# New engine orders and engine choices for windowed attention followed by an RWKV channel mix

## The chip, the cores and the metric

The kernel runs on one core of a Trainium2 chip. The core has TensorE (PE, matmuls), VectorE (DVE), ScalarE (ACT), GpSimd (POOL) and SyncE (SP, which here only issues transfers), and 16 DMA engines that move data between HBM and the on-chip memory SBUF. Matmul results land in PSUM banks. The metric is the device time of one execution in microseconds; a version's time is the median of its runs.

## The reference

Attention over 4 batches, 8 heads, 768 positions and head size 64. Every query sees the 128 newest keys and the first 4 (the sinks). Its output, heads side by side, is the input x of a channel mix with width 512 and hidden width 1024. The core of it:

```python
scores = scale * np.matmul(q, k.transpose(0, 1, 3, 2))
keep = is_sink | in_window
scores = np.where(keep, scores, -1000000000.0)
a = np.exp(scores - np.max(scores, axis=-1, keepdims=True))
a = a / (np.sum(a, axis=-1, keepdims=True) + 1e-09)
attn = np.matmul(a, v)
# x = attn as (B, S, 512); x_prev = x one position earlier
xk = mu_k * x + (1.0 - mu_k) * x_prev
xr = mu_r * x + (1.0 - mu_r) * x_prev
k = np.maximum(xk @ w_k, 0.0)
v = k * k @ w_v
r = 1.0 / (1.0 + np.exp(-(xr @ w_r)))
return r * v
```

Inputs and output are float32 in HBM. The kernel computes in bf16 and accumulates in float32.

## The kernel before

**Tiling.** The 4 x 768 positions are cut into 12 units u of 256 rows, three to a batch, so u = 0, 3, 6, 9 begin a batch. For each unit the functions below append operations to a list, in a fixed order of construction; an operation's place in it is its number (0 to 1030), and those numbers are all that the two tables at the top of the file hold.

- `load` (L386): SP transfers of k, q and v of a unit, into three buffers each. k from unit 4 on and q from unit 8 on come in two halves (L403), the others in one (L410); v comes in halves (L393). `load_weight` (L418): 1 MB each, two for wk, one for wr, two for wv.
- `cast` (L553): a weight to bf16 in pieces of 128 x 1024 (wk four pieces 81 to 84, wr 85 and 86, wv 87 to 90).
- `prepare` (L586): k and q of a unit to bf16 (L594, L597), then transposed so that the head dimension lies on the partitions. Early units do it on PE (four transposes, L623) with an evacuation from PSUM (L631); k from unit 4 on and q from unit 8 on by a transposing transfer on SP (L610). v goes to bf16 (L645). At the start of a batch also the sink keys (L662, POOL) and sink values (L668, L672).
- `attend` (L678): scores of two head pairs at a time in two wide PSUM tiles (L708; for units 0 and 1 a bias is first put there by matmuls, L715), exponentials on ACT (L744), the mask as a product on DVE for units from 2 on (L758), sink scores and their exponentials (L685, L692), values (L770, L782), then reciprocal and scaling into x on DVE (L795, L798).
- `mix` (L807): x transposed on PE (L821), evacuated to xt (L830), the difference of neighbouring positions td (L848), and from it xk and xr (L859).
- `ffn` (L898): keys xk times wk (L909, eight groups of four products), ReLU (L919 or L923), square to kk (L936 or L932), gate xr times wr (L948) and its tanh (L954), kk times wv (L966), the two multiplied into ob (L975) and stored by SP (L982). The last half unit is in two parts (`last_product`, L869).

**What sets the order.** Nothing is scheduled at run time. `ORDER` (L54) lists, for each engine, the numbers of its operations in the order in which the engine runs them, and an engine waits at the head of its list until that operation's inputs and buffers are there. `CHOICE` (L18) gives the engine of an operation that has alternatives: casts of k, q, v (ACT, DVE or POOL), evacuations (ACT or DVE), ReLU and square (ACT or DVE), weight casts. `Plan.schedule` (L163) walks the lists with a table of estimated durations. It decides which buffer each operation takes (four PSUM banks in the pool `bank`, two wide tiles `sc`, five tiles `e`, and so on) and where filler matmuls on a tile of zeros (L986) go into PE's list while it expects PE to be idle, before 32 us of its own clock.

The operations that the prediction speaks of:

| number | what | engine before |
|---|---|---|
| 19; 258, 260 | load of k of unit 3; cast of its first half; its evacuation kt[3,0] | SP; ACT, ACT |
| 259 | PE transposes of k of unit 3, first half | PE |
| 227; 309, 310; 313, 314 | products with wv: unit 0, second half of rows 0 to 127; unit 1, rows 0 to 127 and rows 128 to 255, two halves each | PE |
| 292, 296 | squares kk[1,0], kk[1,1] | ACT, DVE |
| 93, 96; 136 | evacuations kt[0,0], qt[0,0]; kt[1,1] | DVE, ACT; ACT |
| 120, 124; 131 | exponentials of unit 0; cast of q of unit 1 | ACT |
| 158, 159; 161 | bias and scores of unit 1; values of unit 1 | PE |
| 81; 82 | casts of wk, first and second piece | DVE; ACT |
| 206, 207; 210, 211; 214 | keys of unit 0, groups 0, 1 and 2 | PE |
| 234, 192; 175 | sink scores of unit 2; transposes of x of unit 1; values of unit 1 | PE |
| 200; 208, 212; 184; 180 | evacuation of xt; ReLUs of unit 0; cast of k and evacuation kt[2,0] | ACT |
| 236; 317; 443 | scores of unit 2 and of unit 3; first keys of unit 3 | PE |
| 392; 928, 994 | stores of ob of units 2, 9 and 10 | SP |
| 738, 857; 883 | sink keys of the last batch; sink scores of unit 10; cast of q of unit 11 | POOL, PE; ACT |
| 1015, 1019, 1020 | gate and products of unit 11, rows 0 to 127 | PE |

Of the kernel before, what the change touches and what calls it, by code (L numbers as in the profile page):

```python
# [18 lines left out]
    82: "ACT", 83: "ACT", 89: "ACT", 93: "DVE", 97: "DVE", 99: "DVE", 100: "DVE", 102:  # L19
    "DVE", 103: "ACT", 104: "ACT", 133: "DVE", 139: "DVE", 140: "DVE", 141: "DVE", 150:  # L20
    "DVE", 178: "DVE", 181: "DVE", 190: "DVE", 191: "DVE", 209: "ACT", 264: "DVE", 266:
    "DVE", 270: "ACT", 271: "DVE", 283: "DVE", 292: "ACT", 300: "ACT", 341: "DVE", 349:
    "ACT", 352: "DVE", 359: "DVE", 368: "ACT", 372: "ACT", 379: "DVE", 380: "ACT", 417:
    "DVE", 427: "DVE", 428: "DVE", 446: "ACT", 458: "ACT", 495: "POOL", 497: "DVE", 505:
    "DVE", 527: "ACT", 531: "ACT", 535: "ACT", 539: "ACT", 574: "DVE", 581: "DVE", 583:
    "DVE", 584: "DVE", 585: "ACT", 603: "ACT", 660: "ACT", 661: "ACT", 670: "DVE", 679:
    "ACT", 687: "ACT", 728: "DVE", 730: "DVE", 732: "DVE", 736: "ACT", 737: "ACT", 758:
    "ACT", 762: "ACT", 766: "ACT", 770: "ACT", 809: "DVE", 813: "DVE", 814: "ACT", 816:
    "DVE", 823: "DVE", 832: "ACT", 885: "DVE", 890: "ACT", 899: "DVE", 912: "ACT", 915:
    "DVE", 916: "ACT", 920: "ACT", 974: "ACT", 978: "ACT", 986: "ACT", 1002: "ACT", 1006:  # L30
    "ACT", 1013: "DVE", 1014: "ACT",
# [24 lines left out]
        92, 95, 108, 109, 79, 101, 98, 118, 119, 111, 125, 106, 121, 115, 158, 132, 129,  # L56
        142, 135, 138, 159, 182, 149, 156, 188, 168, 169, 165, 234, 161, 175, 206, 207,
        171, 192, 210, 211, 199, 218, 214, 219, 179, 215, 185, 236, 293, 289, 301, 297,
        290, 298, 302, 294, 247, 239, 244, 224, 222, 305, 275, 307, 250, 230, 255, 231,
        226, 282, 262, 227, 259, 268, 309, 317, 265, 310, 313, 342, 328, 314, 365, 369,  # L60
        366, 373, 347, 374, 370, 320, 325, 395, 331, 336, 383, 377, 351, 378, 381, 358,
        273, 393, 406, 385, 389, 420, 386, 390, 443, 425, 451, 444, 452, 398, 473, 409,
        403, 447, 414, 448, 455, 429, 456, 484, 471, 436, 498, 461, 459, 467, 476, 468,
        524, 528, 525, 529, 481, 503, 552, 487, 536, 492, 537, 463, 510, 508, 464, 532,
        517, 563, 533, 555, 540, 560, 542, 548, 577, 549, 586, 600, 604, 601, 566, 605,
        571, 630, 608, 582, 609, 544, 593, 612, 545, 613, 616, 628, 641, 618, 633, 676,
        638, 677, 688, 680, 689, 681, 662, 684, 644, 649, 704, 706, 685, 620, 669, 621,
        624, 717, 694, 625, 755, 692, 756, 759, 763, 709, 760, 764, 714, 783, 720, 696,
        725, 741, 697, 739, 700, 748, 701, 767, 794, 786, 773, 771, 768, 791, 779, 829,
        833, 830, 802, 780, 834, 841, 815, 842, 837, 775, 797, 838, 776, 845, 822, 859,  # L70
        857, 847, 853, 849, 854, 850, 862, 870, 867, 905, 909, 906, 913, 891, 910, 914,
        923, 917, 873, 918, 878, 921, 933, 935, 898, 925, 929, 926, 930, 946, 971, 938,
        943, 972, 975, 979, 976, 980, 957, 983, 949, 984, 954, 987, 989, 964, 995, 991,
        996, 992, 999, 1003, 1000, 1007, 1004, 1011, 1015, 1008, 1012, 1019, 1017, 1020,
# [3 lines left out]
        69, 70, 93, 100, 97, 80, 99, 102, 112, 113, 126, 107, 122, 116, 127, 117, 123,  # L78
        133, 181, 139, 144, 140, 150, 145, 147, 151, 141, 152, 146, 155, 153, 81, 162,
        166, 163, 176, 148, 167, 177, 172, 173, 84, 194, 195, 178, 201, 196, 203, 202,  # L80
        197, 217, 154, 221, 86, 190, 238, 243, 191, 85, 204, 198, 240, 205, 245, 241, 213,
        246, 249, 87, 88, 254, 90, 251, 304, 252, 256, 277, 257, 280, 232, 296, 283, 278,
        284, 228, 264, 279, 281, 288, 341, 266, 286, 319, 285, 324, 311, 315, 335, 271,
        330, 287, 321, 326, 322, 376, 332, 327, 337, 333, 338, 397, 352, 379, 417, 353,
        359, 274, 360, 354, 402, 356, 355, 362, 361, 387, 391, 408, 357, 413, 364, 399,
        400, 410, 404, 411, 405, 363, 497, 415, 454, 416, 427, 431, 450, 475, 434, 432,
        438, 428, 433, 440, 439, 435, 477, 480, 469, 478, 486, 491, 505, 482, 441, 488,
        483, 489, 493, 494, 559, 574, 554, 442, 465, 509, 519, 512, 556, 557, 561, 513,
        562, 514, 521, 520, 565, 515, 550, 570, 581, 567, 523, 568, 572, 584, 516, 573,
        583, 522, 588, 632, 589, 607, 637, 595, 590, 597, 596, 546, 728, 634, 591, 635,  # L90
# [948 lines left out]
```

## Time and profile before

| | |
|---|---|
| median of 8 runs | 167.73 us (167.48 to 168.15) |
| profiled execution, time | 167.32 us |
| profiled execution, span from first to last instruction | 165.4 us |
| PE busy | 157.7 us, 1614 matmuls recorded |
| DVE, ACT busy | 141.8 and 139.4 us |
| POOL busy | 12.7 us |
| moved by DMA | 33.81 MB, mean 204 GB/s |
| TensorE clock granted | full speed in every slice |
| chain that ended last | PE 72%, SP's queue 17%, DMA 7% |

The span is what the profile sees; the time of the same execution is 1.9 us longer. Busy time is the sum of an engine's instructions; for PE their ends are modelled, so gaps are read from the starts. Engines' instructions are named by line, operation and tiles, and a wait is put down to what released it. In the timeline a bracket holds the idle time before a row and who ended it.

### The profile page before, as it was taken

What the parts mean: (1) busy time and instruction counts of PE and PEld (TensorE: products, weight loads), DVE (VectorE), ACT (ScalarE), POOL (GpSimd) and SP (SyncE); (2) the same over time, 40 slices, a digit from 0 to 9 for tenths busy, and PEclk for the clock granted to TensorE, in tenths of its full rate; (3) what the DMA queues carried; (4) which work ended last, traced back from release to release, by engine and by line L of the source; (5) the groups of instructions that cost most, each with busy time, mean ns of one, the idle gap of its engine ahead of it and who ended that gap; (6) DMA issues with size and microseconds to landing.
All of it is one profiled execution on the core that took longest, in us unless ns stands there. A gap on an engine that the chain in (4) does not pass through costs nothing.

```text
span 165.4 us, 4222 instructions
## 1 busy us (share of the span) xinstructions
PE 157.7 (95%) x1614; PEld 107.1 (65%) x1632; DVE 141.8 (86%) x369; ACT 139.4 (84%) x234; POOL 12.7 (8%) x39
## 2 busy tenths in 40 slices
PE   7999789998999999999999999999999999999992
PEld 5657478754577578586585874855765685684761
DVE  5459899999998999999999899889799898978441
ACT  3589999997999999999999899988967799676550
POOL 7800000000100120040000001000000200000000
PEclk9999999999999999999999999999999999999999
DMA  4999999999969989999899698999849952110303
GB/s 139 242 282 256 370 351 266 334 350 270 259 135 283 223 217 234 176 213 251 196 206 235 138 185 245 213 262 261 171 75 258 250 134 111 73 58 0 127 0 127
DMA packets 81762, 33.81 MB, mean 204 GB/s; under 512 B 63688, under 2 KB 76240, under 8 KB 81744
## 3 DMA queue, kind: packets, MB, share of 16 engines
q1 hardware_dynamic: 81728, 33.56, 81.8%
q8 instruction: 12, 0.20, 0.5%
q14 instruction: 6, 0.05, 0.1%
q10 hardware_dynamic: 16, 0.00, 0.0%
HBM read 24.12 MB, written 6.29 MB: 184 GB/s over the span
## 4 chain that ended last, share of the span: by engine, by line
PE 72%; SPq 17%; DMA 7%; issue 1%; ACT 0%; DVE 0%
PE bank L966 22%; PE bank L909 21%; PE bank L948 10%; DMA ks<-in_k_dram 7%; SPq L428 6%; SPq L393 6%; PE sc L708 6%; PE bank L782 5%; SPq L410 4%; PE bank L821 3%; PE bank L770 2%; PE bank L623 2%; PE bank L879 1%; PE bank L685 1%; PE bank L668 0%
## 5 line engine op out<-in xcount | busy, mean ns | idle before, releaser
L909 PE MATMUL bank<-xk,wk_sb 128*128 128x256 bf16 x384 | 49.9, 273 | 0.5 <-DVE wk_sb L565 0.5
L744 ACT ACTIVATE e<-sc 128x1024 bf16<-128x1024 f32 (+1 forms) x48 | 44.6, 964 | 4.7 <-PE sc L708 4.6
L966 PE MATMUL bank<-wv_h,kk 128*128 128x512 bf16 x174 | 43.8, 379 | 0.6 <-issue 0.2
L909 PEld LDWEIGHTS <-wk_sb 128*128 128x128 bf16 x384 | 35.5, 98 | 8.3 <-DVE wk_sb L565 0.6
L919 ACT ACTIVATE rl<-bank 128x512 bf16<-128x512 f32 x45 | 26.1, 606 | 7.2 <-PE bank L909 6.8
L966 PEld LDWEIGHTS <-kk 128*128 128x128 bf16 x184 | 17.0, 98 | 16.2 <-issue 0.2
L758 DVE TENSOR_TENSOR e<-e,mask 128x1024 bf16<-128x1024 bf16 (+1 forms) x40 | 25.7, 653 | 0.1
L948 PE MATMUL bank<-wr_sb,xr 128*128 128x512 bf16 x88 | 23.4, 379 | 0.4
L859 DVE SCALAR_TENSOR_TENSOR xr<-td,mu_all,xt 128x256 bf16<-128x256 bf16 x48 | 23.2, 488 | 0.0
L859 DVE SCALAR_TENSOR_TENSOR xk<-td,mu_all,xt 128x256 bf16<-128x256 bf16 x48 | 21.7, 478 | 0.1
L798 DVE TENSOR_TENSOR x<-bank,rec 128x256 bf16<-128x256 f32 x48 | 19.2, 414 | 0.3
L782 PE MATMUL bank<-vb,e 128*128 128x65 bf16 x352 | 19.5, 193 | 0.0
L782 PEld LDWEIGHTS <-e 128*128 128x128 bf16 x352 | 16.7, 98 | 2.9 <-ACT e L744 0.9
L936 ACT ACTIVATE kk<-rl 128x512 bf16<-128x512 bf16 x29 | 18.0, 631 | 0.6 <-DVE rl L923 0.6
L975 DVE SCALAR_TENSOR_TENSOR ob<-th,bank 128x512 f32<-128x512 f32 x23 | 15.5, 682 | 2.4 <-ACT th L954 1.6
L954 ACT ACTIVATE th<-bank 128x512 f32<-128x512 f32 x24 | 14.2, 603 | 1.4 <-PE bank L948 1.1
L708 PE MATMUL sc<-qt,kt 64*128 64x128 bf16 (+1 forms) x256 | 13.9, 238 | 0.6 <-ACT kt L631 0.4
L795 DVE RECIPROCAL rec<-bank 128x4 f32<-128x4 f32 x48 | 8.2, 176 | 6.7 <-PE bank L782 6.1
L948 PEld LDWEIGHTS <-xr 128*128 128x128 bf16 x96 | 8.6, 98 | 7.8
L770 PE MATMUL bank<-vsink,es 128*128 128x130 bf16 x64 | 12.6, 221 | 0.0
L708 PEld LDWEIGHTS <-kt 64*128 64x128 bf16 x256 | 9.0, 94 | 5.4 <-issue 2.0
L830 ACT COPY xt<-bank 128x512 bf16<-128x512 bf16 x16 | 9.4, 589 | 1.4 <-DVE vsink L672 1.1
(72 smaller groups left out, 172.5 us busy)
## 6 DMA issues: line engine op xcount, KB each, us to landing
vs<-in_v_dram SPq DMA_DIRECT2D x24, 256.0 KB, 4.5
out_dram<-ob SPq DMA_DIRECT2D x23, 256.0 KB, 3.3
ks<-in_k_dram SPq DMA_DIRECT2D x18, 256.0 KB, 4.8
qs<-in_q_dram SPq DMA_DIRECT2D x7, 512.0 KB, 5.7
qs<-in_q_dram SPq DMA_DIRECT2D x10, 256.0 KB, 4.4
w<-in_moe_w_k_dram SPq DMA_DIRECT2D x2, 1024.0 KB, 8.2
w<-in_moe_w_v_dram SPq DMA_DIRECT2D x2, 1024.0 KB, 8.5
ks<-in_k_dram SPq DMA_DIRECT2D x3, 512.0 KB, 8.9
```

What stands on the lines that cost most here:

```text
L708: nc.tensor.matmul(out=sc[:, a, o0:o1], lhsT=lhs[rows], rhs=rhs[rows], start=u not in BIAS, stop=True, skip_group_check=u in BIAS)
L744: nc.scalar.activation(out=buf[ek][:, :, lo:], in_=buf[sck][:, :, lo:], func=AF.Exp, scale=scale)
L758: nc.vector.tensor_tensor(out=at, in0=at, in1=m, op=ALU.mult)
L770: nc.tensor.matmul(out=o[:, g, :, :], lhsT=buf["es", u][:, 128 * g:128 * g + 128], rhs=vsink[b % 2][:, 2 * c:2 * c + 2, :], start=True, st ...
L782: nc.tensor.matmul(out=o[:, g, a, :], lhsT=e[:, a, e0:e0 + 128], rhs=rhs, start=(T == 0 and i == 0), stop=(i == len(blocks) - 1), skip_gro ...
L798: P.op("DVE", dve(256), lambda ok=ok, rk=rk, c=c: nc.vector.tensor_tensor(out=buf["x", u][:, :, 128 * c:128 * c + 128].rearrange("p g (a d ...
L859: nc.vector.scalar_tensor_tensor(out=buf[key][:, c0 + i, :], in0=buf[tk][:, i, :], scalar=mu[w][:, c0 + i:c0 + i + 1], in1=xt[:, c0 + i, t ...
L909: nc.tensor.matmul(out=ps[:, i, :], lhsT=wk_sb[:, c, 128 * f:128 * f + 128], rhs=xk[:, c, :], start=(c == 0), stop=(c == NC - 1), skip_gro ...
L919: nc.scalar.activation(out=buf[rk], in_=buf[psk].rearrange("p (i t) -> p i t", i=2), func=AF.Relu)
L936: nc.scalar.activation(out=buf["kk", u][:, 2 * f2:2 * f2 + 2, :], in_=buf[rk], func=AF.Square)
L948: nc.tensor.matmul(out=buf[psk], lhsT=buf["xr", u][:, c, 128 * g:128 * g + 128], rhs=wr_sb[:, c, :], start=(c == 0), stop=(c == NC - 1))
L966: nc.tensor.matmul(out=buf[psk], rhs=wv_h[:, f, :], lhsT=buf["kk", u][:, f, 128 * g:128 * g + 128], start=(f == 0), stop=(f == NF - 1))
```

## The change

Both tables are replaced. No other line differs: the operations, their dependences, the tiles and the loops are the same, so each engine runs the same kinds of instructions on the same shapes. 75 operations change their engine: 29 casts of q, k and v, one weight cast (81), 15 evacuations, 5 ReLUs and 25 squares. Most trade places between ACT and DVE (31 go to DVE, 32 to ACT; of the squares 12 and 13); ten casts go to POOL, seven from ACT and three from DVE, and two leave POOL. ACT has 230 operations after 235, DVE 354 after 357, POOL 24 after 16; PE (307) and SP (116) have the same ones in another order. The diff, cut within the long lists:

```diff
 CHOICE = {
-    82: "ACT", 83: "ACT", 89: "ACT", 93: "DVE", 97: "DVE", 99: "DVE", 100: "DVE", 102:
-    "DVE", 103: "ACT", 104: "ACT", 133: "DVE", 139: "DVE", 140: "DVE", 141: "DVE", 150:
-    "DVE", 178: "DVE", 181: "DVE", 190: "DVE", 191: "DVE", 209: "ACT", 264: "DVE", 266:
-    "DVE", 270: "ACT", 271: "DVE", 283: "DVE", 292: "ACT", 300: "ACT", 341: "DVE", 349:
-    "ACT", 352: "DVE", 359: "DVE", 368: "ACT", 372: "ACT", 379: "DVE", 380: "ACT", 417:
-    "DVE", 427: "DVE", 428: "DVE", 446: "ACT", 458: "ACT", 495: "POOL", 497: "DVE", 505:
-    "DVE", 527: "ACT", 531: "ACT", 535: "ACT", 539: "ACT", 574: "DVE", 581: "DVE", 583:
-    "DVE", 584: "DVE", 585: "ACT", 603: "ACT", 660: "ACT", 661: "ACT", 670: "DVE", 679:
-    "ACT", 687: "ACT", 728: "DVE", 730: "DVE", 732: "DVE", 736: "ACT", 737: "ACT", 758:
-    "ACT", 762: "ACT", 766: "ACT", 770: "ACT", 809: "DVE", 813: "DVE", 814: "ACT", 816:
-    "DVE", 823: "DVE", 832: "ACT", 885: "DVE", 890: "ACT", 899: "DVE", 912: "ACT", 915:
-    "DVE", 916: "ACT", 920: "ACT", 974: "ACT", 978: "ACT", 986: "ACT", 1002: "ACT", 1006:
-    "ACT", 1013: "DVE", 1014: "ACT",
+    81: "POOL", 82: "ACT", 83: "ACT", 89: "ACT", 93: "DVE", 96: "DVE", 99: "DVE", 100:
+    "DVE", 103: "DVE", 104: "ACT", 134: "POOL", 136: "DVE", 137: "DVE", 139: "DVE", 140:
+    "ACT", 141: "ACT", 143: "DVE", 150: "DVE", 178: "DVE", 187: "POOL", 189: "DVE", 190:
+    "DVE", 191: "DVE", 258: "DVE", 271: "DVE", 283: "DVE", 292: "ACT", 296: "ACT", 304:
+    "ACT", 341: "DVE", 343: "DVE", 344: "DVE", 349: "ACT", 352: "DVE", 359: "DVE", 368:
+    "ACT", 376: "ACT", 380: "ACT", 417: "POOL", 424: "POOL", 427: "ACT", 428: "DVE", 430:
+    "DVE", 446: "ACT", 454: "ACT", 458: "ACT", 495: "POOL", 497: "DVE", 506: "DVE", 535:
+    "ACT", 539: "ACT", 579: "DVE", 584: "DVE", 585: "ACT", 594: "DVE", 607: "ACT", 611:
+    "ACT", 615: "ACT", 652: "POOL", 660: "ACT", 661: "ACT", 663: "DVE", 687: "ACT", 691:
+    "ACT", 728: "DVE", 730: "DVE", 732: "DVE", 736: "DVE", 737: "ACT", 758: "ACT", 766:
+    "ACT", 770: "ACT", 813: "DVE", 814: "DVE", 816: "DVE", 832: "ACT", 836: "ACT", 840:
+    "ACT", 844: "ACT", 881: "DVE", 883: "POOL", 887: "POOL", 889: "ACT", 890: "ACT", 892:
+    "DVE", 899: "DVE", 920: "ACT", 974: "ACT", 982: "ACT", 1002: "ACT", 1005: "DVE", 1006:
+    "ACT", 1009: "DVE", 1010: "ACT", 1014: "ACT",
 }
...
     "PE": (
-        92, 95, 108, 109, 79, 101, 98, 118, 119, 111, 125, 106, 121, 115, 158, 132, 129,
-        142, 135, 138, 159, 182, 149, 156, 188, 168, 169, 165, 234, 161, 175, 206, 207,
-        171, 192, 210, 211, 199, 218, 214, 219, 179, 215, 185, 236, 293, 289, 301, 297,
-        290, 298, 302, 294, 247, 239, 244, 224, 222, 305, 275, 307, 250, 230, 255, 231,
-        226, 282, 262, 227, 259, 268, 309, 317, 265, 310, 313, 342, 328, 314, 365, 369,
-        366, 373, 347, 374, 370, 320, 325, 395, 331, 336, 383, 377, 351, 378, 381, 358,
-        273, 393, 406, 385, 389, 420, 386, 390, 443, 425, 451, 444, 452, 398, 473, 409,
-        403, 447, 414, 448, 455, 429, 456, 484, 471, 436, 498, 461, 459, 467, 476, 468,
...
-        943, 972, 975, 979, 976, 980, 957, 983, 949, 984, 954, 987, 989, 964, 995, 991,
-        996, 992, 999, 1003, 1000, 1007, 1004, 1011, 1015, 1008, 1012, 1019, 1017, 1020,
+        95, 92, 108, 109, 98, 101, 79, 106, 118, 119, 111, 115, 121, 132, 158, 129, 125,
+        142, 138, 159, 149, 156, 182, 188, 135, 168, 169, 161, 165, 175, 171, 234, 192,
+        210, 206, 211, 199, 207, 218, 214, 219, 179, 215, 185, 236, 289, 301, 297, 290,
+        302, 298, 293, 247, 294, 239, 222, 244, 224, 305, 275, 255, 307, 230, 250, 231,
+        226, 262, 282, 227, 313, 259, 309, 268, 317, 265, 314, 310, 342, 328, 373, 365,
+        347, 366, 369, 374, 370, 320, 325, 395, 336, 381, 331, 377, 351, 378, 383, 358,
+        393, 406, 389, 385, 273, 386, 420, 390, 443, 425, 451, 444, 452, 398, 447, 409,
+        473, 403, 448, 455, 414, 456, 429, 484, 471, 436, 461, 459, 467, 498, 468, 476,
...
+        979, 972, 975, 943, 976, 980, 949, 983, 957, 984, 989, 954, 987, 991, 964, 995,
+        992, 996, 999, 1003, 1000, 1004, 1007, 1011, 1008, 1012, 1017, 1019, 1015, 1020,
     "DVE": (
-        69, 70, 93, 100, 97, 80, 99, 102, 112, 113, 126, 107, 122, 116, 127, 117, 123,
-        133, 181, 139, 144, 140, 150, 145, 147, 151, 141, 152, 146, 155, 153, 81, 162,
-        166, 163, 176, 148, 167, 177, 172, 173, 84, 194, 195, 178, 201, 196, 203, 202,
-        197, 217, 154, 221, 86, 190, 238, 243, 191, 85, 204, 198, 240, 205, 245, 241, 213,
-        246, 249, 87, 88, 254, 90, 251, 304, 252, 256, 277, 257, 280, 232, 296, 283, 278,
-        284, 228, 264, 279, 281, 288, 341, 266, 286, 319, 285, 324, 311, 315, 335, 271,
-        330, 287, 321, 326, 322, 376, 332, 327, 337, 333, 338, 397, 352, 379, 417, 353,
-        359, 274, 360, 354, 402, 356, 355, 362, 361, 387, 391, 408, 357, 413, 364, 399,
...
+        69, 70, 96, 93, 100, 103, 99, 80, 112, 113, 137, 122, 116, 123, 117, 107, 126,
+        143, 127, 139, 144, 147, 150, 145, 151, 136, 146, 153, 148, 152, 162, 166, 163,
+        189, 176, 167, 177, 172, 155, 173, 154, 84, 194, 195, 178, 201, 196, 202, 203,
+        197, 209, 213, 204, 85, 86, 221, 190, 238, 191, 243, 300, 240, 205, 241, 198, 245,
+        254, 246, 217, 88, 87, 249, 90, 256, 277, 251, 257, 252, 278, 232, 258, 283, 280,
+        284, 228, 286, 279, 344, 285, 288, 287, 341, 319, 315, 311, 343, 324, 281, 271,
+        335, 330, 321, 326, 322, 337, 327, 338, 332, 372, 333, 352, 402, 353, 397, 359,
+        354, 356, 360, 355, 361, 362, 274, 387, 391, 363, 408, 364, 413, 399, 410, 400,
...
     "ACT": (
-        68, 67, 91, 94, 96, 114, 110, 103, 104, 124, 120, 131, 137, 128, 134, 130, 143,
-        187, 160, 164, 183, 136, 157, 189, 174, 235, 170, 82, 208, 193, 83, 200, 212, 184,
-        180, 216, 220, 186, 237, 242, 291, 299, 209, 295, 303, 248, 225, 253, 223, 276,
-        306, 89, 308, 261, 267, 292, 258, 263, 300, 260, 339, 269, 318, 323, 344, 346,
-        343, 334, 270, 329, 367, 348, 375, 371, 396, 368, 384, 401, 372, 382, 419, 422,
...
-        936, 920, 922, 941, 952, 947, 973, 977, 981, 958, 985, 978, 974, 988, 986, 965,
-        990, 1001, 1002, 1005, 1006, 1009, 1014, 1016, 1018,
+        68, 67, 94, 91, 97, 114, 110, 102, 104, 120, 131, 124, 128, 133, 130, 181, 164,
+        160, 140, 183, 141, 157, 174, 170, 82, 235, 193, 83, 200, 208, 184, 212, 180, 220,
+        186, 216, 242, 237, 291, 303, 299, 295, 253, 248, 223, 225, 306, 276, 89, 296,
+        308, 261, 292, 267, 263, 264, 304, 260, 339, 269, 318, 266, 323, 346, 334, 329,
+        348, 367, 375, 371, 368, 401, 382, 396, 376, 379, 422, 380, 394, 384, 419, 412,
...
+        952, 947, 973, 977, 981, 974, 958, 982, 985, 988, 965, 990, 1001, 1002, 1006,
+        1013, 1010, 1014, 1016, 1018,
     "POOL": (
-        72, 71, 76, 73, 77, 75, 78, 74, 105, 272, 350, 495, 506, 507, 738, 889,
+        72, 71, 78, 76, 77, 75, 73, 105, 74, 134, 187, 81, 272, 270, 417, 424, 350, 495,
+        505, 507, 652, 883, 738, 887,
     "SP": (
-        0, 1, 3, 2, 4, 5, 7, 6, 16, 10, 11, 8, 9, 15, 12, 17, 18, 13, 14, 20, 19, 23, 25,
-        24, 233, 21, 22, 340, 345, 28, 30, 29, 312, 26, 27, 229, 418, 423, 33, 35, 31, 34,
-        32, 316, 36, 496, 501, 37, 38, 39, 470, 40, 45, 41, 388, 575, 43, 580, 44, 49, 42,
-        46, 392, 50, 653, 655, 657, 51, 659, 47, 52, 729, 733, 48, 466, 547, 53, 731, 735,
-        55, 627, 54, 57, 551, 58, 59, 63, 56, 623, 699, 61, 806, 808, 812, 810, 60, 703,
-        64, 65, 62, 778, 66, 882, 884, 782, 888, 886, 856, 852, 928, 932, 998, 994, 1022,
-        1030, 1026,
+        1, 0, 2, 3, 4, 5, 7, 6, 16, 10, 11, 8, 9, 15, 12, 17, 18, 13, 14, 20, 19, 23, 24,
+        25, 233, 21, 22, 340, 345, 28, 29, 30, 229, 26, 27, 312, 418, 423, 33, 35, 392,
+        34, 31, 32, 36, 496, 38, 501, 39, 37, 316, 40, 45, 575, 388, 43, 580, 41, 46, 466,
+        44, 42, 49, 655, 659, 51, 653, 657, 50, 52, 47, 48, 551, 731, 547, 729, 733, 735,
+        53, 57, 470, 54, 55, 56, 59, 808, 699, 627, 623, 58, 806, 63, 810, 812, 61, 62,
+        782, 60, 703, 64, 884, 882, 886, 888, 65, 778, 856, 66, 852, 932, 998, 994, 928,
+        1022, 1030, 1026,
```

## The prediction

> **What bounds the kernel now.** I read the waits first, then TensorE (PE) in order of time, then the queues that feed it. PE is busy for 157.7 of 165.4 us, but the ends of matmuls are modelled, so I do not take that share as proof. The list of waits, asked for PE alone, is better evidence:
>
> ```profile
> PE bank L986 <- DVE warm L1002: 1.1, 1, 1.1
> PE bank L623 <- ACT kb L597: 0.6, 1, 0.6
> PE bank L623 <- DVE xt L830: 0.5, 1, 0.5
> PE bank L909 <- DVE wk_sb L565: 0.5, 1, 0.5
> PE sc L708 <- ACT kt L631: 0.4, 1, 0.4
> PE bank L966 <- issue: 0.2, 1, 0.2
> ```
>
> That is every named wait of PE: 3.3 us, of which 1.1 is the start. The timeline of PE puts the four that matter at 17.03, 18.76, 21.49 and 41.29 us:
>
> ```profile
> 17.03 0.38 PE L623 MATMUL bank<-ident,qb 128*128 128x128 bf16 x4 [0.54 <-DVE xt L830]
> ...
> 18.76 0.62 PE L708 MATMUL sc<-qt,kt 64*128 64x256 bf16 x12 [0.38 <-ACT kt L631]
> ...
> 21.49 1.05 PE L909 MATMUL bank<-xk,wk_sb 128*128 128x256 bf16 x8 [0.46 <-DVE wk_sb L565]
> ...
> 39.66 1.03 PE L966 MATMUL bank<-wv_h,kk 128*128 128x512 bf16 x4
> 41.29 0.40 PE L623 MATMUL bank<-ident,kb 128*128 128x128 bf16 x4 [0.60 <-ACT kb L597]
> ```
>
> After about 46 us there is none. The chain of waits agrees: `153.40 2.62 PE bank L909 x24` is 24 starts 109 ns apart, and `149.94 3.45 PE bank L966 x16` is 16 at 216 ns, so PE issues at its steady step there. From 46 us to the last matmul at 161.8 the kernel is the sum of its matmuls, and an order can't shorten that. What an order can win lies before 46 us, and it can lose anywhere.
>
> The wait at 41.29 is the largest, and the chain shows its cause:
>
> ```profile
> 29.24 11.35 DMA ks<-in_k_dram
> 40.62 0.63 ACT kb L597
> 41.29 0.62 PE bank L623 x8
> ```
>
> The reader sees a load of k (operation 19, k of unit 3) that takes 11.35 us to land, its cast on ScalarE, and the transposes (259). The trace has 16 completion counts for each load: for this one the fifteenth came at 39.73 us and the last at 40.59. One DMA engine of 16 was 0.86 us behind. The same split stands at both loads of wk (19.82 and 20.71; 22.54 and 23.48). Each comes a few us after a 16 KB packet on the instruction queue (14.54, 37.26 us; 1.28 and 1.19 us long; 12 such in the run). The Trainium skill (Runtime: NRT & Kernel Launch, "Instruction fetch mechanics") says of such a fetch that its cost is "mostly hidden", which would price it at nothing. The row decides here: the load's last count ends a PE wait of 0.77 us (previous step ended 40.52, start 41.29).
>
> **The change, part by part.** I label operations by their number in the two lists; u is a unit of 256 rows.
>
> *PE at 40 us.* Before, 259 follows 227 directly. After, 313 (four products of kk[1] with wv, 4 x 216 ns = 0.86 us) stands between. 313 needs casts of wv that end by 35.95, kk[1,0] (39.63 before) and kk[1,1] (39.96 before), and both move earlier on ScalarE, behind 89 and 261; I get 38.1 and 39.7 for them, against a start at 41.0. So the wait of 0.77 us is filled with work that is due anyway: **-0.77 us**. The k load is issued at the same place in SP's list, and the cast 258 moves from ScalarE to VectorE (40.62 plus 0.42 instead of 0.62), so 259 is ready at 41.1 and not wanted before 41.8. What is late next is kt[3,0] and scores 317; ScalarE makes it by 42.9, as before (42.73).
>
> *The first 27 us, a chain of small waits that moves.* I walked the queues with start-to-start steps of the rows (ScalarE 0.5 us per 512 columns, 0.93 per exponential of 1024; VectorE 0.34 to 0.60; PE as above), against the recorded landings. (a) Start: k and q of head half 0 swap, and both evacuations (96, 93) go to VectorE, 0.69 us each in turn; the first scores slip 0.1, and the second scores still start at 10.2. (b) ScalarE casts q (131) between two exponentials, so the score banks come free 0.5 later: 158 moves from 12.70 to 12.9, and 159 waits for kt[1,0] at 15.0 anyway (15.11 before). Nothing. (c) The waits at 17.03 and 18.76: 136 leaves ScalarE for VectorE, kt[1,1] is there by 18.5 instead of 18.70, but values 161 then wait for es[1] and vb[1,1], both now on ScalarE, until 19.5 (19.30 before): +0.1 in all. (d) The wait at 21.49: keys 210 now come first, on wk[1], which ScalarE casts after its two exponentials, 21.3 plus 1.07 = 22.4; PE has by then done the scores 234 and the transposes 192 in place of 206 and 207. Level within 0.1. (e) At 24.8, 214 takes the fifth PSUM bank after 175, and that is the one that 200 empties at 25.05: +0.35. Then 236 waits for kt[2,0], which ScalarE reaches at 27.2 behind 208, 184 and 212 (26.76 before). So 236 starts at 27.25, not 26.82: **+0.43**, of which none is won back before 40 us, since PE has no gap there. The walk is good to some 0.4 us; between 0 and +0.7 I take +0.4, by the two rows that end it.
>
> *wk[0] on POOL (81).* The row nearest is a POOL cast of half the size: 0.62, 0.64, 0.90 and 1.25 us. Twice that is 1.2 to 2.5 us from the landing at 20.71, so 21.9 to 23.2, wanted by 206 at 22.8: 0 to +0.4, I take 0, for three of four rows lie at the short end.
>
> *Ten casts to POOL, two away from it.* VectorE's moves without that add up to -1.8 us (25 squares, 12 to it and 13 away at 0.41, and so on) and ScalarE's to -3.0 us. But a POOL cast isn't free for VectorE:
>
> ```profile
> 56.66 0.64 POOL L645 CAST vb<-vs 128x512 bf16<-128x512 f32 x1 [11.27 <-DMA vs<-in_v_dram]
> ...
> 56.75 0.83 DVE L859 SCALAR_TENSOR_TENSOR xr<-td,mu_all,xt 128x256 bf16<-128x256 bf16 x1
> 57.50 0.47 DVE L859 SCALAR_TENSOR_TENSOR xk<-td,mu_all,xt 128x256 bf16<-128x256 bf16 x1
> ```
>
> The operation beside the cast took 0.83 us, the next one of its kind 0.47: 0.36 lost. The Trainium skill (SBUF — State Buffer, "SBUF: two separate sides") says that the pair of ports is locked for a whole instruction and the other engine fully blocks. By that rule a cast may cost VectorE its own length, 0.62 to 1.25; by the row 0.36, because the two overlap only in part and VectorE also has operations that read PSUM. Eight more casts, one of them double, make nine: 9 x 0.36 = 3.2 us by the row, up to 9 x 0.9 = 8 by the rule. I take the row. VectorE then has 1.4 us more, not 1.8 less, and ScalarE 3.0 less. Where it falls matters: 46 to 85 us has four casts more net, 1.4 us, less 0.4 moved away. VectorE is busy there for 37.5 of 39 us and ScalarE for 38.3, so +1.0 just fits beneath 1.5 us of idle. Cost on PE: 0.
>
> *The rest of the orders.* PE's changes of array mode go from 59 to 60, the extra one late; a score group after other products starts about 0.1 us later than the step of the products (312 ns after a product of 216), so **+0.1**. On SP, stores move against loads (store 392 right behind load 35, before loads 34, 31, 32, 36): it waits for ob[2,1], 59.96 before, and holds those loads some 1.5 us. k of unit 6 is next wanted for scores at 72.4 and its transposes ran at 65.1 to 69.2, so 3 us of cover hide it. Store 928 goes behind 994, off the end. POOL's 738 (sink keys, wanted by 857 at about 127 us) stands behind the cast 883, whose load now lands by about 120: 7 us of cover. The last eight products and what follows them (the end is 3.6 us behind the last matmul) keep their order but for 1015, which moves behind 1019; its gate is wanted after 1020, and ScalarE has it by 160.2. Nothing.
>
> Sum: -0.77 + 0.4 + 0.1 = -0.3 us. The profiled execution took 167.32 us with a span of 165.4, the median of the eight runs is 167.73, so I carry the difference over to that: **167.4 us**. What a measurement of this kernel tells from no change is about 0.2%, 0.34 us, so the forecast stands on that edge.
>
> **Rivals.** *All four early waits go.* If (c), (d) and (e) come out as the order seems to want and not as I walked them, 0.54 + 0.38 + 0.46 + 0.77 = 2.1 us are there; I credit two thirds, 1.4: 166.3. For it: in each place something ready was put ahead of the waiter. Against: the sum of ScalarE and VectorE work before 27 us is hardly less, so the chain only moves.
>
> *The lock decides.* Each POOL cast costs VectorE not 0.36 but 0.6 us or more: between 46 and 85 us that is 4 x 0.6 - 0.4 = 2.0 against 1.5 us of idle, and from there on PE waits, first at keys 443 (VectorE ended xk[3,2] at 58.77, the product started at 58.86) and values after masks. At the rule's 0.9 it is 3.2 - 1.5 = 1.7 us late, less the forecast's 0.3: 169.1; at the middle, 168.5. For it: VectorE's operations with two SBUF inputs fill most of its time there. Against: the trace has 0.36 and once 0.39.
>
> *Given back.* The 0.77 us is won and lost again: wk[0] at 23.2 (+0.4) and the walk's +0.7: 167.73 - 0.77 + 1.1 = 168.0, or about 167.8 with one of them. In this rival the change does not do what it says, as far as time goes.
>
> **How the numbers follow.** Forecast 0.55 (of it faster 0.30, within 0.2% 0.17, slower 0.08, by the walk's 0.4 us). All early waits 0.15, all faster. Lock 0.20, all slower. Given back 0.10: faster 0.02, same 0.05, slower 0.03. Together faster 0.47, same 0.22, slower 0.31. The likeliest case alone is 166.9 to 167.9; with half of each outer rival the range is 166.2 to 168.7.
>
> **What would show it.** Right: no PE wait ahead of the transposes 259 at 41 us, with 313 in its place; 236 a few tenths later than 26.82; PE waits after 46 us still absent; POOL casts of 0.6 to 1.3 us with a VectorE operation some 0.36 longer beside each. Wrong: a named PE wait on VectorE between 55 and 85 us, or 236 well before 26.8, or filler products (L986) beyond 12 us, which the order of before does not have.

## The result, and the profile after

The changed kernel took 166.79 us, the median of 20 runs (166.19 to 167.95), against 167.97 us for the kernel before in 55 runs beside it (166.89 to 169.43). The ratio is 0.9934, with a 95% interval of 0.9918 to 0.9949; ratios here leave out slow executions, those over 1.5% above the fastest of their kernel. The forecast was 167.4 us. The change is faster, by 1.1 us, about three times what was summed.

The two profiled executions are much closer to each other: 167.32 and 166.78 us, spans 165.4 and 165.1. From the trace I give a few starts on PE that split the difference. "Cut" is the first product of the keys of unit 2 (operations 365 and 373); up to there both orders have done the same set of 79 PE operations.

| profiled execution | 236 | 259 | cut | last matmul | cut to last |
|---|---|---|---|---|---|
| before | 26.82 | 41.29 | 46.81 | 161.82 | 115.01 |
| after | 27.43 | 41.99 | 46.55 | 161.54 | 114.99 |

Of the 0.28 us on PE, 0.26 is there at the cut. The rest of the 0.54 us lies behind the last matmul and outside the span (1.9 against 1.7 us). The list of PE's named waits in the changed kernel (waited for, us in total, times, longest):

```profile
PE bank L987 <- DVE warm L1003: 1.1, 1, 1.1
PE bank L624 <- ACT qb L598: 0.9, 1, 0.9
PE bank L624 <- ACT kb L598: 0.7, 2, 0.5
PE bank L669 <- DVE vb L646: 0.6, 1, 0.6
PE bank L783 <- ACT e L745: 0.5, 2, 0.3
PE bank L624 <- DVE xt L831: 0.4, 1, 0.4
PE bank L624 <- DVE qb L598: 0.3, 1, 0.3
PE bank L910 <- ACT xt L831: 0.2, 1, 0.2
PE bank L967 <- issue: 0.2, 1, 0.2
```

There is more named waiting than before (4.9 us against 3.3), not less, and it is other waiting: the waits for kt and for wk are not in this list, and waits for casts of q, k and v stand in their place. It fits with the fillers, which I did not count: 23 in place of 35, which take 4.9 us from start to start in place of 6.6. Time that a filler covers and time that is named as a wait are the same loss. The timeline of PE (start, length, engine and line, operation, count) shows the two places that the prediction turned on:

```profile
26.97 0.39 PE L624 MATMUL bank<-ident,kb 128*128 128x128 bf16 x4
27.43 0.62 PE L709 MATMUL sc<-qt,kt 64*128 64x256 bf16 x12
...
40.04 0.39 PE L822 MATMUL bank<-ident,x 128*128 128x128 bf16 x4
40.27 1.89 PE L967 MATMUL bank<-wv_h,kk 128*128 128x512 bf16 x8
41.99 0.39 PE L624 MATMUL bank<-ident,kb 128*128 128x128 bf16 x4
42.22 1.03 PE L967 MATMUL bank<-wv_h,kk 128*128 128x512 bf16 x4
```

At 27.43 the scores 236 start, 0.6 late. At 40.27 stand eight products and not four: the second four are 313, and the transposes 259 follow at 41.99 with no bracket, so without a wait. The casts on POOL and what VectorE did beside them:

```profile
21.14 1.04 POOL L566 CAST wk_sb<-w 128x1024 bf16<-128x1024 f32 x1 [5.12 <-DMA w<-in_moe_w_k_dram]
51.27 0.61 POOL L595 CAST kb<-ks 128x512 bf16<-128x512 f32 x1 [3.51 <-DMA ks<-in_k_dram]
55.08 0.68 POOL L598 CAST qb<-qs 128x512 bf16<-128x512 f32 x1 [3.20 <-DMA qs<-in_q_dram]
```

```profile
50.98 0.72 DVE L799 TENSOR_TENSOR x<-bank,rec 128x256 bf16<-128x256 f32 x2
...
54.81 0.48 DVE L860 SCALAR_TENSOR_TENSOR xk<-td,mu_all,xt 128x256 bf16<-128x256 bf16 x1
55.20 0.83 DVE L860 SCALAR_TENSOR_TENSOR xr<-td,mu_all,xt 128x256 bf16<-128x256 bf16 x1
```

Beside the cast at 55.08 xr takes 0.83 in place of 0.48 us. The two operations that read a PSUM bank overlap each other and take 0.39 and 0.42 us; the second runs wholly beside the cast at 51.27, and the group's mean is 0.415. All fourteen profiled executions below say the same. Of 117 VectorE operations that read PSUM and ran for over 0.1 us beside a POOL cast, none was more than 0.01 us longer than is usual for its kind. Of 115 with two bf16 inputs in SBUF (xr, xk, the mask product and a few others), 46 were longer by 0.1 to 0.43 us. The loss goes with the neighbour. VectorE's busy time is 141.1 us (141.8 before), ScalarE's 137.3 (139.4), POOL's 16.3 (12.7).

### The profile page after: what moved, and what is told of

Its sections match the earlier page's. It is cut to its first block, busy times and chain, and to the rows that moved or that the text cites. A ratio compares the mean times of both kernels' runs of the same rounds, so it can differ in the third digit from the quotient of the medians.

```text
span 165.1 us, 4192 instructions
## 1 busy us (share of the span) xinstructions
PE 155.7 (94%) x1601; PEld 105.7 (64%) x1620; DVE 141.1 (85%) x366; ACT 137.3 (83%) x229; POOL 16.3 (10%) x47
## 4 chain that ended last, share of the span: by engine, by line
PE 81%; SPq 8%; DMA 5%; issue 2%; ACT 2%; DVE 0%
PE bank L967 24%; PE bank L910 24%; PE bank L949 13%; PE sc L709 6%; PE bank L783 6%; DMA w<-in_moe_w_k_dram 5%; SPq L394 4%; SPq L411 3%; PE bank L822 3%; PE bank L771 2%; PE bank L624 2%; PE bank L880 1%; SPq L429 1%; PE bank L686 1%; ACT rl L920 1%
## 5 line engine op out<-in xcount | busy, mean ns | idle before, releaser
L910 PE MATMUL bank<-xk,wk_sb 128*128 128x256 bf16 x384 | 49.2, 273 | 0.2 <-ACT xt L831 0.2
L967 PE MATMUL bank<-wv_h,kk 128*128 128x512 bf16 x172 | 44.3, 379 | 0.7 <-issue 0.2
L920 ACT ACTIVATE rl<-bank 128x512 bf16<-128x512 f32 x46 | 26.6, 608 | 10.9 <-PE bank L910 9.5
L937 ACT ACTIVATE kk<-rl 128x512 bf16<-128x512 bf16 x30 | 18.6, 631 | 0.3 <-DVE rl L924 0.2
L849 DVE TENSOR_TENSOR td<-xt 128x512 bf16<-128x512 bf16 x24 | 10.1, 420 | 0.9 <-ACT xt L831 0.8
```

The costliest lines, as they stand in the source:

```text
L910: nc.tensor.matmul(out=ps[:, i, :], lhsT=wk_sb[:, c, 128 * f:128 * f + 128], rhs=xk[:, c, :], start=(c == 0), stop=(c == NC - 1), skip_gro ...
L920: nc.scalar.activation(out=buf[rk], in_=buf[psk].rearrange("p (i t) -> p i t", i=2), func=AF.Relu)
L937: nc.scalar.activation(out=buf["kk", u][:, 2 * f2:2 * f2 + 2, :], in_=buf[rk], func=AF.Square)
L967: nc.tensor.matmul(out=buf[psk], rhs=wv_h[:, f, :], lhsT=buf["kk", u][:, f, 128 * g:128 * g + 128], start=(f == 0), stop=(f == NF - 1))
```

## The experiments

Two questions were open: in which part of the orders the time lies, and why the runs differ by 1.1 us when the profiles differ by 0.5. Twelve runs followed, three of them copies. This table has them all; "k1" is when the last of the 16 completion counts of the load of k for unit 1 (operation 6) came, and all columns from "profiled" on are of the one profiled execution.

| kernel | runs | median us | ratio to before, 95% interval | profiled us | k1 | cut | cut to last matmul |
|---|---|---|---|---|---|---|---|
| before | 55 | 167.97 | | 167.32 | 13.08 | 46.81 | 115.01 |
| after | 20 | 166.79 | 0.9934 [0.9918, 0.9949] | 166.78 | 13.48 | 46.55 | 114.99 |
| before_2 | 12 | 168.00 | 0.9971 [0.9946, 0.9996] | 167.91 | 13.50 | 47.38 | 115.05 |
| after_2 | 6 | 166.56 | 0.9919 [0.9887, 0.9950] | 166.51 | 13.00 | 46.25 | 115.00 |
| h_early | 12 | 168.14 | 0.9972 [0.9940, 1.0004] | 167.29 | 12.90 | 46.33 | 115.32 |
| h_early_2 | 12 | 167.45 | 0.9978 [0.9952, 1.0004] | 167.37 | 12.88 | 46.23 | 115.49 |
| h_mid | 12 | 168.25 | 1.0006 [0.9975, 1.0036] | 166.90 | 13.03 | 46.16 | 114.98 |
| h_late | 12 | 168.57 | 0.9994 [0.9968, 1.0020] | 168.70 | 14.15 | 47.80 | 115.04 |
| b_313 | 12 | 168.17 | 0.9976 [0.9944, 1.0009] | 167.44 | 13.24 | 46.65 | 115.33 |
| a_no313 | 12 | 167.50 | 0.9939 [0.9903, 0.9975] | 167.55 | 13.89 | 46.87 | 115.43 |
| b_shift | 12 | 167.99 | 1.0008 [0.9985, 1.0031] | 168.05 | 14.26 | 47.54 | 115.04 |
| a_shift | 12 | 167.46 | 0.9980 [0.9955, 1.0005] | 167.03 | 12.99 | 46.79 | 114.98 |
| b_long | 12 | 168.18 | 0.9996 [0.9973, 1.0019] | 167.94 | 13.17 | 46.47 | 115.94 |
| a_long | 12 | 167.82 | 0.9960 [0.9935, 0.9986] | 166.75 | 12.94 | 46.49 | 114.99 |

The medians are compared through the ratio, since each batch had its own chip: the kernel before has medians of 167.88 to 168.43 us in the four batches of experiments, and a ratio is not the quotient of two medians of the table. The copy before_2 sets how finely: the same code reads 0.9971. I take nothing within 0.3% of 1 as a difference. The profiled execution is one of the runs. It is the lowest of its twelve in h_early and h_mid and the second lowest in b_313, a_shift and a_long, so the last four columns flatter these.

**Early or late?** One kernel takes the new engines and orders for the first 46 us (PE's first 79 operations, SP's first 29, and what they need), the other for the rest.

```diff
 # h_early: both tables joined at the cut; h_late the other way round
     "PE": (
-        92, 95, 108, 109, 79, 101, 98, 118, 119, 111, 125, 106, 121, 115, 158, 132, 129,
+        95, 92, 108, 109, 98, 101, 79, 106, 118, 119, 111, 115, 121, 132, 158, 129, 125,
...
-        226, 282, 262, 227, 259, 268, 309, 317, 265, 310, 313, 342, 328, 314, 365, 369,
+        226, 262, 282, 227, 313, 259, 309, 268, 317, 265, 314, 310, 342, 328, 365, 369,
         366, 373, 347, 374, 370, 320, 325, 395, 331, 336, 383, 377, 351, 378, 381, 358,
```

> The new orders and engines for what runs in the first 46 us, the old ones for the rest. Early theory (the gain is the filled wait for the k load of unit 3, which in most executions is longer than the 0.77 us of the profiled one): nearly the whole gain, 0.7 to 1.1 us below the kernel before, and no PE wait ahead of the transposes 259. Late theory (the old order has products after 46 us that are ready only just in time, such as keys 443 with 0.1 us, and loses there in executions that no profile showed): 0.3 us below at most.

> The old orders and engines for the first 46 us, the new ones for the rest. Early theory: level with the kernel before, within 0.3 us, the wait at 41 us still there. Late theory: 0.6 to 1.0 us below the kernel before, with that wait still there.

h_early reached the cut at 46.33, as early as the changed kernel, then took 0.3 us longer to the last matmul; its ratio of 0.9972 is that of a copy, though the interval reaches down to 0.9940. h_late needed 115.04 us behind the cut, the same as the old late orders in the profile before. So in these profiles the late orders win nothing, and the early ones alone are not shown to bring the timed gain. Neither half brought what the theory named after it expected. h_late also shows what the old early orders do when a load lands late. Its PE timeline:

```profile
13.25 0.39 PE L624 MATMUL bank<-ident,qb 128*128 128x128 bf16 x4
14.85 0.40 PE L624 MATMUL bank<-ident,kb 128*128 128x128 bf16 x4 [1.21 <-ACT kb L598]
```

The transposes of k of unit 1 wait 1.21 us for the cast; the fifteenth count of that load came at 12.81 and the last at 14.15. A 16 KB packet on the instruction queue (a fetch of instructions) started at 13.84, when the last count was already 1.0 us behind, so it is not shown to be the cause. In the profile before these transposes started at 13.87. The cut comes at 47.80, not 46.81.

**The one swap at 40 us, alone.**

```diff
 # b_313
...
-        226, 282, 262, 227, 259, 268, 309, 317, 265, 310, 313, 342, 328, 314, 365, 369,
+        226, 282, 262, 227, 313, 259, 268, 309, 317, 265, 310, 342, 328, 314, 365, 369,
 # a_no313
...
-        226, 262, 282, 227, 313, 259, 309, 268, 317, 265, 314, 310, 342, 328, 373, 365,
+        226, 262, 282, 227, 259, 313, 309, 268, 317, 265, 314, 310, 342, 328, 373, 365,
```

> The kernel before with one number moved: products 313 stand before the transposes 259 on PE. Early theory: 0.6 to 1.0 us below the kernel before, since 313 is ready (its last input at 39.96 us) and fills the wait. Late theory: the wait goes, but at most 0.3 us of it reaches the end.

> The kernel after with 313 put back behind 259. Early theory: PE waits some 0.5 us or more ahead of 259 again and the kernel is 0.5 to 0.8 us slower than after. Late theory: 0.3 us slower than after at most, so still 0.8 us below the kernel before.

Doing it alone gives 0.9976, undoing it in the changed kernel leaves 0.9939: not distinguishable from nothing in either. In a_no313 there is no wait at 259, because PE comes there later (41.45) and k of unit 3 is cast in time (40.78). The two terms of the sum, -0.77 for this wait and +0.4 for coming late, overlap: what comes late does not wait.

The profiles say more than the medians here. From 236 to the cut a_no313 takes 19.13 us without the swap, as the changed kernel does with it (19.12); b_313 takes 19.92 with it (before: 19.99), since 0.40 us goes at 37.8 to a wait for a piece of wv. In the changed kernel the cast of k of unit 3 ended at 40.74, and without 313 PE would have come to 259 at about 41.13. So in that execution there was no wait there for 313 to fill. By the same sum 313 fills some 0.3 us in a_shift, where the load landed at 41.15.

**A second run of two kernels, and the place of the instruction fetches.** Copies of the changed kernel and of h_early, and both kernels with each filler of 256 columns given as two of 128. The time of the fillers stays, PE's instructions are 31 pairs (22 in the changed kernel) more, and the first 16 KB fetch moves from 14.5 to 11.8 us (from 15.0 to 12.5).

```diff
 # b_shift, a_shift
-    P.fill = lambda bank, half: nc.tensor.matmul(
-        out=bank[:, 0:256] if half else bank, lhsT=warm[:, 0:128], start=True, stop=True,
-        rhs=warm if half else warm.unsqueeze(1).to_broadcast([128, 2, 256]))
+    def fill_with(bank, half):
+        if half:
+            for c in range(2):
+                nc.tensor.matmul(out=bank[:, 128 * c:128 * c + 128], lhsT=warm[:, 0:128], start=True,
+                                 stop=True, rhs=warm[:, 0:128], skip_group_check=True)
...
+    P.fill = fill_with
```

> The kernel after once more, for a second profiled execution and to stand on the same chip as the next three. All theories: about 0.993 of the kernel before. The place of the late counts of single loads after a 16 KB fetch may differ from the first profile by 1 us or more.

> The first-46-us hybrid once more (new orders early, old ones late), for a narrower interval. Early theory: within 0.3 us of the kernel after. Late theory: 0.5 us or more slower than after, on the same chip.

> The kernel before with every small filler matmul of 256 columns as two of 128, so that PE runs some 30 more matmuls and as many more weight loads in its first 9 us and reaches each 16 KB fetch some 2 to 3 us earlier, with no other edit. Fetch theory (a fetch leaves one DMA engine about 1 us behind until SP's queue runs dry, and what waits for that engine's part pays): the first late counts move to the loads of unit 1 that land at 11 to 13 us, a wait of about 1 us appears on PE before 15 us, and the time rises by 0.5 to 1 us. If the place of a fetch does not matter: within 0.3 us of the kernel before.

> The same edit in the kernel after (23 fillers instead of 35, so the fetch moves by some 1.5 to 2 us). Fetch theory: slower than after by less than the same edit costs the kernel before, 0 to 0.5 us, since its casts of unit 1 have more behind them. If the place of a fetch does not matter: within 0.3 us of after.

after_2 repeats the gain (0.9919). h_early_2 reads 0.9978, and its median is 0.9 us above that of after_2 on the same chip, as the late theory had it. b_shift moves the fetch onto the load of k of unit 1 (last count 1.57 us behind the fifteenth), its cut comes at 47.54, and its profiled 168.05 us is 0.7 above the profile before; yet its median is that of the kernel before (1.0008). Either the ordinary executions of the kernel before are already as late as this, or the later fetches, which move as well, give something back; the next batch bears on that. a_shift has a profile 0.25 us above that of the changed kernel and loses about 0.6% of ratio against after_2 on the same chip, most of the gain and more than was expected.

**Fewer fillers, and the kernel before once more.** The opposite edit, fillers of 256 columns in pairs as one of 512, puts the first fetch at 14.9 and 16.1 us. For b_long that is no later than in before_2, which has it at 15.5 with no edit at all, so b_long does not test the place of the first fetch.

```diff
 # b_long, a_long
+    halves = []
+
+    def fill_with(bank, half):
+        if half:
+            halves.append(1)
+            if len(halves) % 2 == 0:
+                return
+        nc.tensor.matmul(out=bank, lhsT=warm[:, 0:128], start=True, stop=True,
+                         rhs=warm.unsqueeze(1).to_broadcast([128, 2, 256]))
```

> A copy of the kernel before, for a second profile. If the profile on record (167.32 us, first keys of unit 2 at 46.81) was a favourable execution, this one has a PE wait of about 1 us between 13 and 14.5 us, first keys of unit 2 at 47.3 to 47.8 us and a time near 168. If it was an ordinary one, the first keys come at 46.8 again and the difference between 167.32 and the median lies behind 46 us. Ratio 1.000 in both.

> The kernel before with its 31 filler matmuls of 256 columns taken in pairs as one of 512, so some 15 matmuls and 15 weight loads fewer and the first 16 KB instruction fetch later. If ordinary executions of the kernel before lose about 1.2 us because that fetch falls just ahead of the landing of k of unit 1, the fetch moves from 13.8 to 14.5 us to about 15 or later, PE has no wait over 0.7 us between 13 and 15 us, the first keys of unit 2 start at about 46.7 us and the median falls by 0.3 to 0.8 us: 0.995 to 0.998. If the place of the fetch decides nothing and the gain of the changed kernel is its orders alone: 1.000, within 0.002.

> The changed kernel with its 22 fillers of 256 columns taken in pairs, so some 11 matmuls and 11 loads fewer. If the place of the first fetch decides, it comes at about 15.5 us, later than k and q of unit 1 have landed, the first keys of unit 2 start at 46.0 to 46.3 us and the ratio to before is 0.989 to 0.992, at or below that of the changed kernel. If only the orders count: 0.992 to 0.9935, the same as the changed kernel.

before_2 bears on the first point. The same code as before, 167.91 us, close to its median; PE's timeline at the places whose waits the prediction showed:

```profile
15.27 0.62 PE L708 MATMUL sc<-qt,kt 64*128 64x256 bf16 x12
...
17.46 0.38 PE L623 MATMUL bank<-ident,qb 128*128 128x128 bf16 x4 [0.71 <-DVE xt L830]
...
22.16 1.05 PE L909 MATMUL bank<-xk,wk_sb 128*128 128x256 bf16 x8 [0.81 <-DVE wk_sb L565]
...
27.50 0.62 PE L708 MATMUL sc<-qt,kt 64*128 64x256 bf16 x12
```

These waits were 0.54 and 0.46 us in the first profile, and 236 started at 26.82. The expectation had a single wait of about 1 us; there is none. The loads land later (k1 13.50 in place of 13.08, wk[0] 21.39 in place of 20.71), these two waits are 0.17 and 0.35 us longer, and the cut comes 0.57 us later. So the first profile, 0.16 us below the lowest of the eight runs beside it, was a favourable execution.

b_long did not get the lower median of its expectation (0.9996). Its early part did get faster, with the cut at 46.47, and the wait at 259 is gone with the old orders and no swap, for PE comes there 0.43 us later than before and the cast ends 0.33 us earlier:

```profile
39.93 1.03 PE L966 MATMUL bank<-wv_h,kk 128*128 128x512 bf16 x4
40.95 0.40 PE L623 MATMUL bank<-ident,kb 128*128 128x128 bf16 x4
```

The last count of load 19 came at 40.26 there, 0.30 us behind the fifteenth (0.86 before). In all fourteen profiled executions this lag goes with the place of the third 16 KB fetch. In the six in which it starts at 34.8 to 38.0 us (before, before_2, h_late, b_313, b_shift, a_shift) the lag is 0.55 to 1.28 us; in the eight in which it starts at 38.1 to 39.4 it is 0.03 to 0.37. Orders alone do not make the two groups: b_long with old orders stands in the second and a_shift with new ones in the first, each by its fillers. So whether PE waits at 259 hangs also on where a fetch falls, and the changed kernel, with twelve fillers fewer, has that fetch 1.9 us later (39.13 against 37.26).

b_long then lost 0.9 us behind the cut where the profile before shows none. ScalarE first, then PE:

```profile
64.79 0.60 ACT L919 ACTIVATE rl<-bank 128x512 bf16<-128x512 f32 x1
66.67 0.62 ACT L594 CAST kb<-ks 128x512 bf16<-128x512 f32 x1 [1.28 <-DMA ks<-in_k_dram]
67.20 0.38 ACT L692 ACTIVATE es<-bank 128x256 bf16<-128x256 f32 x1
```

```profile
65.86 1.03 PE L948 MATMUL bank<-wr_sb,xr 128*128 128x512 bf16 x4
67.63 1.02 PE L948 MATMUL bank<-wr_sb,xr 128*128 128x512 bf16 x4 [0.73 <-ACT es L692]
```

ScalarE stands 1.28 us at the cast 500 of k of unit 6, whose load (34) is late; the small exponential es behind it frees PE's bank, and PE stands too. The same cast in the changed kernel:

```profile
65.26 0.64 ACT L595 CAST kb<-ks 128x512 bf16<-128x512 f32 x1
```

No bracket. I then read, in every profiled execution, how long load 34 had landed when its cast began. Where the old orders run in this stretch from the cut on (before, before_2, b_313, b_shift, b_long, h_early, h_early_2) it is 0.02 to 0.03 us, seven times of seven: the cast starts the moment the load is there, at 65.84 to 66.69. PE lost by it 0.90 in b_long, 0.17 in h_early_2 and 0.07 in b_313, three of the four that reached the cut before 46.7, and nothing where the cut came later. With the new orders up to here the cover is 0.07 in after, 0.93 in after_2, 0.48 in h_mid, 0.25 in a_long, 0.14 in h_late, but 0.02 in a_shift and 0.03 in a_no313. a_no313 even stands 1.07 us on ScalarE at this cast and loses 0.17 on PE, and its ratio is that of the changed kernel. A possible reason stands in SP's list: before, load 31 is issued ahead of 34; after, it is behind it. But h_mid has the old list here and a cover of 0.48, so that is not all. In after, 34 is issued at 60.40 and lands 4.8 us later; before, at 59.52 and 6.3 us later.

a_long has a profile as good as the changed kernel's (166.75 us), but its median is 1.07 us above that profile. Its ratio, 0.9960, is 0.26% above that of the changed kernel, which is within what a copy shows.

**The seam moved.** If the late orders hold part of the gain, a joint at 59 us, behind the place at 49 us where h_early lost 0.3, should not help; if the early part is all, it should.

```diff
 # h_mid: the tables joined behind PE's first 106 operations and SP's first 40
     "SP": (
-        0, 1, 3, 2, 4, 5, 7, 6, 16, 10, 11, 8, 9, 15, 12, 17, 18, 13, 14, 20, 19, 23, 25,
-        24, 233, 21, 22, 340, 345, 28, 30, 29, 312, 26, 27, 229, 418, 423, 33, 35, 31, 34,
+        1, 0, 2, 3, 4, 5, 7, 6, 16, 10, 11, 8, 9, 15, 12, 17, 18, 13, 14, 20, 19, 23,
+        24, 25, 233, 21, 22, 340, 345, 28, 29, 30, 229, 26, 27, 312, 418, 423, 33, 35,
+        31, 34, 32, 316, 36, 496, 501, 37, 38, 39, 470, 40, 45, 41, 388, 575, 43, 580,
...
```

> The new orders and engines up to about 58.8 us (PE's first 106 operations, SP's first 40), the old ones behind, so the seam of h_early at 46 us is moved behind the place where it cost 0.3 to 0.5 us. If all of the gain is in the first 46 us: first keys of unit 2 at 46.2 to 46.6 us, last matmul 115.0 to 115.3 us behind them, and a ratio of 0.992 to 0.995, as the changed kernel. If the new orders behind 59 us hold part of it, by losing less in executions in which a load lands late: a ratio of 0.997 to 1.000 as h_early had, though the profiled early part is as fast.

The profiled execution is the best one of a hybrid: cut at 46.16, 114.98 us behind it, 166.90 us. And it is the lowest of its twelve runs; the median is 168.25, the ratio 1.0006. Of the two theories only the second, that the orders behind 59 us hold part of the gain in executions the profile did not catch, allows about this ratio. A third, that a joint of two orders costs something by itself, was not tested.

## Why the prediction was right, and where it was off

**The wait at 41.29 (-0.77).** Right as an event: 313 runs there, 259 doesn't wait. From 236 to the cut the changed kernel takes 19.12 us in place of 19.99, so the size is right too, -0.87. The cause is not the swap alone. It was not needed for it (a_no313: 19.13 without it), and b_long has no such wait with neither swap nor new orders (19.39). Without 313 PE would have come to 259 some 0.6 us later than before, and the cast ended 0.5 us earlier: 0.3 by the load and the rest by VectorE's shorter cast. The wait depends on how late the last count of load 19 is, and that goes with the third fetch. The prediction took the fetch for a fixed part of the picture; the change moved it. As a cause of the timed gain the swap is not shown: b_313 and a_no313 can't tell it from zero.

**The walk to 27 us (+0.4).** 236 came at 27.43, +0.61, inside 0 to +0.7. But that execution had k1 at 13.48; after_2, with k1 at 13.00 and so nearest to the landings I walked against, has 27.13, +0.31. Over all profiles 236 starts at 27.22 us on average in the six with old early orders (26.73 to 27.65) and at 27.30 in the eight with new ones (27.03 to 27.74). So +0.4 was a loss against one early execution, and about +0.1 against several.

**wk[0] on POOL.** Cast 1.04 us long, ended at 22.18, at the short end of 21.9 to 23.2; the first of its products run in the group at 22.55, with no named wait there. Nothing, as taken.

**The lock (nine casts at 0.36, 3.2 us).** Too large. The durations of VectorE's operations add up to 166.5 us before and 164.8 after, 1.7 less, nearly the 1.8 that the moves alone give; busy time fell by only 0.7 because they overlap less. In both kernels three operations beside a POOL cast are longer, by 1.1 us in all, so the added casts cost VectorE nothing that can be seen. The row was right for an xr beside a cast (0.83 against 0.48), but most casts fell beside other work. The rival in which the lock decides fell: VectorE is busy 37.3 us between 46 and 85, against 37.5 before, and no PE wait on it stands there. The Trainium skill (SBUF — State Buffer, "SBUF: two separate sides") was weighed at up to 8 us, and the runs show neither that nor my 3.2. The same section names the operations that can be blocked by a POOL operation that reads SBUF, those in a two-port mode or with two SBUF inputs. I left that list out and charged every cast. The lengthened operations here all have two SBUF inputs.

**Late orders (+0.1; SP's moves hidden with 3 us of cover).** Cut to last matmul: -0.02 in the first two profiles. The cover was wrong. I looked for it at PE, where k of unit 6 is wanted late. It is wanted first by ScalarE, whose queue stands still at its cast, and there it was 0.02 us in the very profile I read. That it cost nothing before and nothing after hid the mistake.

**A sign of error that did come.** One filler well beyond 12 us, at 16.04, in time that PE had idle. It proves little, since the order before has one too, at 12.05, which the prediction missed.

**The sum.** -0.37 at the cut and +0.1 behind it, rounded to -0.3; the first two profiles give -0.28 at the last matmul. That agreement is partly luck, for they are unlike executions: before with k1 at 13.08, after at 13.48. At like landings the new orders reach the cut earlier by 0.56 us (46.25 against 46.81, at 13.00 and 13.08) or 0.83 us (46.55 against 47.38, at 13.48 and 13.50). Over all fourteen profiles, variants included, the cut comes at 47.11 us on average with old early orders and at 46.46 with new ones, 0.65 earlier.

**The step that failed** is the last one: "I carry the difference over" to the median. The profile before lies 0.65 us below the median of 55 runs, the profile after at its own. A sum made against one execution holds for that execution's landings. For two that lie at their medians, before_2 and after, 167.91 and 166.78 us, the difference is 1.13 us, as in the runs, and 0.83 us of it stands at the cut. They come from different batches, and medians of the same code differ by up to 0.5 us between batches, so this agreement is a sign and not a proof.

**What stays open.** h_early and h_mid reach the cut as early as the changed kernel, and their medians do not show it. In h_early_2, whose profile is near its median, 0.5 us goes behind the cut: 0.30 at 49.3 us, where values wait, and 0.17 at the cast 500. In h_mid nothing is lost in the one execution that was recorded, and 1.35 us more is spent in the middle of its twelve. Where, no trace here shows. That it is again a load without cover would fit with the cast 500, but is argued, not shown. So is the reason why more fillers cost the changed kernel 0.6% (a_shift) and the kernel before nothing (b_shift); it would fit with orders that suit one placing of the twelve fetches, but no run placed a fetch by itself. No kernel here beat the changed one.

## What to carry to other kernels

Before a sum is carried from a profile to a median, compare the profiled time with the runs: here it lay 0.4 us below the median of the eight runs shown, and below each of them, and that was a sign that its landings were early. Read the cover of a load at the first in-order queue that stops for it, not at the engine that is short. Ask of a wait for a late load what made the load late, before crediting a swap that fills it: here edits of the fillers alone moved the fetch, and with it the load's last count. When a change wins time early, look at which late loads had no cover, since a load that is issued by a queue of its own does not land sooner because TensorE comes sooner.

## What the runs showed of the hardware

- **A late last count goes with the place of a fetch.** Each profiled execution has 12 or 13 packets of 16 KB on the instruction queue. The last of the 16 counts of wk[0] lags the fifteenth by 0.49 to 1.25 us in the eleven executions whose first packet starts at 14.4 to 16.1 us, and by 0.02 to 0.08 in the three that have it at 11.8 to 13.8. In after, with packets at 15.0, 26.7, 39.1, 51.1 us and so on, it is 1.22 us at the four loads that land at 18.4, 21.1, 23.8 and 25.6. For the third packet and load 19 the lags are given above. Not every lag is explained so: k1 lags by 0.61 us in after, before any packet. The Trainium skill (Runtime: NRT & Kernel Launch, "Instruction fetch mechanics") has the cost "mostly hidden"; what was not hidden shows in the 0.77 us that PE lost at 41.29 in the kernel before, behind a last count 0.86 us late.
- **The place of a fetch follows the instructions.** 31 matmuls and 31 weight loads more in the first 12 us brought the first one to 11.8 us, from 14.5 and 15.5 in two executions of the kernel before.
- **The same code differs by landings.** Two profiled executions of the kernel before differ by 0.42 us at the load of k of unit 1, by 0.68 at wk[0], and by 0.57 at the cut.
- **A POOL cast costs VectorE by its neighbour:** up to 0.43 us for an operation with two SBUF inputs beside it (46 of 115 were longer by over 0.1), at most 0.01 us for one that reads PSUM (117 cases).
